# First batch's first MLP: two token pieces of 256 and 320, or two halves of 288 in one tile over two PSUM banks

## The chip, the cores and the metric

The kernel runs on one core of one Trainium2 chip. The metric is device time in microseconds of one execution, the median over several. Five engines work side by side, each in the order of its own queue: TensorE (PE, with its weight loads as PEld), VectorE (DVE), ScalarE (ACT), GpSimd (POOL) and SyncE (SP), which issues most of the DMAs.

## What is computed

Three layers follow each other over 4 batches of 576 tokens, so 2304 tokens in all:

```
k_m, v_m = softmax(phi)^T k, softmax(phi)^T v        per batch and head: 32 memory rows
attn     = softmax(q k_m^T / 8) v_m                  8 heads of 64 -> x of width 512
h        = x @ w_in                                  512 -> 2048
x2       = (h * sigmoid(h)) @ w_out                  2048 -> 512
out      = top-2 of 8 experts over x2, each relu(x2 @ w1[e]) @ w2[e], weighted by the routing
```

The change lies in the second layer, the first MLP, of the first batch only. All values are fp32; a matrix product is made of three products of fp32r parts, high by high, high by low and low by high.

## The kernel before

**Stages.** The first batch's attention comes first. Then the first MLP runs over the batches in steps, and the attention of the next batch, the projection of w_in through v_m, and the routing are hung between the steps as hooks. After the fourth batch the experts run to the end. The weights w_in and w_out arrive as 64-bit values, and during the first batch they are narrowed to fp32 on ACT, DVE and POOL (lines 209 to 232) and split into high and low parts (lines 263, 264, 275, 276). So the first batch's steps carry work on these three engines that later batches don't have.

**A step of the first MLP.** A step s belongs to batch s // 32 and to a block f of 128 rows of the 2048 hidden ones. Each block has two steps, i = 0 with tokens 0 to 255 and i = 1 with tokens 256 to 575. `mlp_h` (line 280) makes 6 matmuls into a PSUM tile `h` of one bank, of which there are two (line 288). Then ACT makes a tanh from PSUM (line 291), DVE multiplies and adds with a second read of PSUM (line 293), which gives twice h * sigmoid(h), ACT copies 256 columns as the high part `gh` (line 297) and DVE or POOL subtracts it for the low part `gl` (line 298). In the first batch POOL has this subtraction in every fourth step, that is for i = 0 of the even blocks. The last 64 tokens of i = 1 go to `gc` the same way (lines 306, 307). When line 293 is done, PE may write that bank again.

**The second product.** `mlp_x` (line 316) runs LAG = 4 steps later and takes block f's `gh` and `gl` as moving data of 512 columns: 6 matmuls a step at line 313, into four PSUM banks that are held for the whole batch. Two more banks, `aux`, serve everything else, so that all 8 are taken.

**Order.** The kernel is written step by step (the loop at the end of `body`: `run_x`, `run_h`, then the hooks), and a scheduler then sets each engine's order from the program, the buffers and its own costs. `issue_after` pins a few places. On the chip each engine runs its list strictly in order.

Of the kernel before, what the change touches and what calls it, by code (L numbers as in the profile page):

```python
# [6 lines left out]
F32 = mybir.dt.float32  # L7
F32R = mybir.dt.float32r
# [3 lines left out]
AF = mybir.ActivationFunctionType  # L12
OP = mybir.AluOpType
AX = mybir.AxisListType

B, H, S, D, M = 4, 8, 576, 64, 32
# [13 lines left out]
MAIN = 512  # L30
NOWHERE = 65536
LAG = 4
# [12 lines left out]
def body(ctx, tc, a):  # L45
    nc = tc.nc
    pe, act, dve, pool, sp = nc.tensor, nc.scalar, nc.vector, nc.gpsimd, nc.sync

    const = ctx.enter_context(tc.tile_pool(name="const", bufs=1))
    ps = ctx.enter_context(tc.tile_pool(name="ps", bufs=2, space=bass.MemoryType.PSUM))  # L50
# [2 lines left out]
    tab_d = tc.dram_tile([E * NS, 2], I32, name="tab_d")  # L53
    xs_d = [tc.dram_tile([CAP, DM], F32, name=f"xs_d{i}") for i in range(2)]

    def psum(tag, bufs):
        return ps.tile([128, 512], F32, name=tag, tag=tag, bufs=bufs)

    ji = const.tile([128, 128], I32, name="ji")
    pool.iota(ji, pattern=[[1, 128]], base=0, channel_multiplier=-1)  # L60
# [15 lines left out]
    m1 = moe1.enter_context(tc.tile_pool(name="m1", bufs=1))  # L76
# [3 lines left out]
    QT, KV, KX, PH, KVT, AH, AU = {}, {}, {}, {}, {}, {}, {}  # L80
# [34 lines left out]
    def phi_max(b, g):  # L115
        r = slice(g * 128, (g + 1) * 128)
        pt = psum("aux", 2)
        pe.transpose(pt[:, :SC], MX.pop((b, g)), ident)
        mt = ap_.tile([128, 1], F32, name="mt")
        dve.tensor_reduce(mt, pt[:, :SC], axis=AX.X, op=OP.max)  # L120
        pb = psum("aux", 2)
        pe.matmul(pb[:SC, :128], mt.to_broadcast([128, SC]), ident, start=True, stop=True)
        for c0, c1 in ((0, 2), (2, NCH)):
            e = PH[b][:, c0:c1, r]
            dve.tensor_sub(e, e, pb[:SC, None, :128].to_broadcast([SC, c1 - c0, 128]))
            last = act.activation(e, e, AF.Exp)
        return last

    def memory(b, g):
        pk = psum("aux", 2)  # L130
        for c in range(NCH):
            for h in range(4):
                j = (4 * g + h) * M

                kv = KV[b, 2 * g + h // 2][:, c, h % 2, :] if c < 4 else KX[b, g][:, h % 2, :]
                pe.matmul(pk[h * M:(h + 1) * M, :130], PH[b][:, c, j:j + M], kv, start=(c == 0), stop=(c == NCH - 1))
        rs = ap_.tile([128, 1], F32, name="rs", bufs=2)
        dve.tensor_scalar(rs, pk[:, 128:129], 1e-9, None, op0=OP.add)
        dve.reciprocal(rs, rs)
        v, w = src[:, :, g, :], pk[:, :128].rearrange("p (t d) -> p t d", t=2)  # L140
        if b == 0:
            act.activation(v, w, AF.Copy, scale=rs)
        else:
            dve.tensor_scalar(v, w, rs, None, op0=OP.mult)
# [90 lines left out]
    WP, WI, ST = {}, {}, {}  # L235
# [42 lines left out]
    G, X2, GC = {}, {}, {}  # L278

    def mlp_h(b, f, i):  # L280
        t0, w = T0[i], TW[i]
        hi, lo = WP[(b * NP + f // 2) // 2]
        c = (f % 4) * 128
        p = psum("h", 2)
        n = 0
        for g in range(2):
            for wt, at in ((hi, 0), (hi, 1), (lo, 0)):
                pe.matmul(p[:, :w], wt[:, g, c:c + 128], AH[b, g][at][:, t0:t0 + w], start=(n == 0), stop=(n == 5))  # L288
                n += 1
        th = m1.tile([128, 320], F32, name="th", bufs=2)  # L290
        act.activation(th[:, :w], p[:, :w], AF.Tanh, scale=0.5)  # L291
        u = th
        dve.scalar_tensor_tensor(u[:, :w], th[:, :w], 1.0, p[:, :w], op0=OP.add, op1=OP.mult)  # L293
        if i == 0:
            G[b, f] = [m1.tile([128, MAIN], F32R, name=f"g{x}", bufs=LAG // 2 + 1) for x in "hl"]
        gh, gl = (x[:, i * 256:(i + 1) * 256] for x in G[b, f])
        act.activation(gh, u[:, :256], AF.Copy)  # L297
        last = (pool if b == 0 and (2 * f + i) % 4 == 0 else dve).tensor_sub(gl, u[:, :256], gh.bitcast(F32))  # L298
        if b:
            LATEST[0] = last  # L300
        if i == 1:
            if (b // 2, f) not in GC:
                GC[b // 2, f] = [m1.tile([128, 128], F32R, name=f"gc{f}_{x}") for x in range(2)]
            ch, cl = GC[b // 2, f]
            r = slice((b % 2) * 64, (b % 2) * 64 + 64)
            act.activation(ch[:, r], u[:, 256:], AF.Copy)
            dve.tensor_sub(cl[:, r], u[:, 256:], ch[:, r].bitcast(F32))

    def accumulate(key, terms, f):
        if f == 0:  # L310
            X2[key] = psum("x2", 4)
        for n, (held, moved) in enumerate(terms):
            pe.matmul(X2[key], held, moved, start=(f == 0 and n == 0), stop=(f == NF - 1 and n == 2))  # L313
# [575 lines left out]
    def at(s, fn, *args):  # L889
        hooks.setdefault(s, []).append((fn, args))  # L890
# [6 lines left out]
    for f in range(1, NF):  # L897
        at(max(0, 2 * f - 5), fetch_wout, f)
        at(2 * f - 1, narrow_wout, f)
    SB = 2 * NF  # L900
    at(8, routing_setup)
    for b in range(1, B):
        s = (b - 1) * SB
        at(s + (1 if b > 1 else 4), load_phi, b)
# [25 lines left out]
        for i in range(0, NP, 2):  # L930
            for x in range(2):
                at(s + SB - 8 + 4 * i, fetch_win, b * NP + i + x)
            at(s + SB - 4 + 4 * i, project, b * NP + i, 2)
    for b in range(B - 1):
        s = (b + 1) * SB + LAG
        for d in range(4):
# [5 lines left out]
        if b == 1:  # L942
# [3 lines left out]
            at(s + 6, tile_d, j)  # L946
    s = 3 * SB
    at(s, open_a)
    at(s - SB + 10, clear)
    for j in range(EARLY):  # L950
# [4 lines left out]
    total = B * SB  # L955
# [1 line left out]
        mlp_x(s // SB, s % SB // 2, s % 2)  # L957

    def run_h(s):
        if s < total:  # L960
            mlp_h(s // SB, s % SB // 2, s % 2)

    def run_hooks(s):
# [16 lines left out]
    s = 0  # L980
    while s < total + LAG + 6:
        if LAG <= s < total + LAG:
            run_x(s - LAG)
        run_h(s)
        run_hooks(s)
        if s in (2 * SB, 4 * SB):
            b = s // SB - 1
            for i in range(1, LAG):
                run_x(s - LAG + i)
                run_hooks(s + i)  # L990
                if s == total and i > 1:
                    main_a(b, 2 * i - 4)
                    main_a(b, 2 * i - 3)
            if s < total:
                cut = (0, 2, 6, 11, NF)
                for i in range(1, LAG + 1):
                    mlp_rest(b, range(cut[i - 1], cut[i]))
                    if i < LAG:
                        run_h(s + i)
                tile_a(TILES.index((b, 4)))  # L1000
                run_hooks(s + LAG)
            else:
                mlp_rest(b, range(0, 2))
                main_c(b)
                mlp_rest(b, range(2, 4))
                main_d(b)
                mlp_rest(b, range(4, 10))
                late = gate(13, 17)()
                late(13, 15)
                for g in range(2):  # L1010
                    main_rows(b, g)
                mlp_rest(b, range(10, NF))
                for fn in (tile_a, tile_b, tile_c, tile_d):
                    fn(17)
            s += LAG - 1
# [55 lines left out]
```

## Time and profile before

| what | us |
|---|---|
| median of 3 runs (845.02 to 845.68) | 845.61 |
| the profiled execution, its own time | 845.91 |
| its span, first to last instruction | 844.1 |
| PE busy in the span | 807.1 (96%) |
| DVE busy | 496.8 (59%) |
| ACT busy | 360.8 (43%) |
| POOL busy | 209.9 (25%) |

A busy share is an average over stages with different limits. PE's matmuls overlap, so that a PE that is busy all the time need not be one at its peak. In the trace a matmul of the change's kind stands at line 288, its tanh at 291, the multiply-add at 293, copy and subtraction at 297 and 298, those of the last 64 tokens at 306 and 307, and the second product at 313.

### The profile page before, as it was taken

The numbers are of one execution on the slowest core, as the hardware profiler recorded it, in microseconds if no ns is written. First come the engines' busy times: TensorE is split into PE (matmuls) and PEld (weight loads), VectorE is DVE, ScalarE is ACT, GpSimd is POOL, SyncE is SP. The second block draws the span as 40 slices with busy tenths as digits, with TensorE's granted clock in tenths as the row PEclk, the third lists the DMA queues.
The fourth block names the chain that finished last, engine by engine and source line by source line (L and its number), as shares of the span: only waits on it lengthen the run. The fifth ranks groups of instructions, "written<-read, shape, count | busy, mean of one in ns | idle before, by whom it ended". The sixth has DMA issues, their size and how long they took to land.

```text
span 844.1 us, 14185 instructions
## 1 busy us (share of the span) xinstructions
PE 807.1 (96%) x5260; PEld 691.4 (82%) x5260; DVE 496.8 (59%) x1178; ACT 360.8 (43%) x856; POOL 209.9 (25%) x237
## 2 busy tenths in 40 slices
PE   4589999999999999999999999999999999999996
PEld 2267678878887888887988989989989899898995
DVE  4898996884268747655724555354553654546521
ACT  3689975444333454553414433324332333233410
POOL 1254530021000400400541504215133142241301
PEclk9599999999999999999999999999999999999999
DMA  9889852543074215232456893765748647586201
GB/s 304 291 295 325 283 217 71 159 131 94 7 229 153 51 51 151 57 82 50 113 138 187 257 257 124 185 237 171 188 169 221 241 139 160 198 220 196 74 4 53
DMA packets 85935, 137.84 MB, mean 163 GB/s; under 512 B 14045, under 2 KB 48349, under 8 KB 85856
## 3 DMA queue, kind: packets, MB, share of 16 engines
q1 hardware_dynamic: 74656, 104.41, 40.9%
q0 software_dynamic: 11200, 32.43, 12.7%
q8 instruction: 43, 0.70, 0.4%
q14 instruction: 36, 0.29, 0.1%
HBM read 106.13 MB, written 31.26 MB: 163 GB/s over the span
## 4 chain that ended last, share of the span: by engine, by line
PE 81%; DVE 9%; ACT 4%; DMA 3%; issue 2%; POOL 1%; SPq 0%; POOLq 0%; ACTq 0%; DVEq 0%
PE x L706 25%; PE x L313 18%; PE x L682 13%; PE h L682 12%; PE h L288 9%; PE aux L157 2%; DMA st<-moe_w_out 1%; DVE th L293 1%; DVE gl L298 1%; DMA kx<-kx 1%; ACT lw L211 1%; POOL wo L232 1%; DMA st<-moe_w_in 1%; DVE mx L113 1%; DVE wo L217 1%
## 5 line engine op out<-in xcount | busy, mean ns | idle before, releaser
L706 PE MATMUL x<-w,gh 128*128 128x512 f32 (+1 forms) x608 | 188.1, 390 | 0.0
L706 PEld LDWEIGHTS x<-w,gh 128*128 128x128 f32 (+1 forms) x608 | 112.4, 186 | 24.3
L682 PE MATMUL h<-xh,w 128*128 128x304 f32 (+4 forms) x512 | 118.7, 304 | 0.0
L706 PE MATMUL x<-w,gl 128*128 128x512 f32 (+1 forms) x304 | 118.5, 390 | 0.0
L682 PE MATMUL x<-xh,w 128*128 128x304 f32 (+4 forms) x512 | 118.1, 302 | 0.0
L288 PE MATMUL h<-ah,wph 128*128 128x320 f32 (+1 forms) x512 | 109.3, 302 | 3.8 <-DVE th L293 1.7
L313 PE MATMUL x<-gh,woh 128*128 128x512 f32 x256 | 105.5, 412 | 0.0
L288 PEld LDWEIGHTS h<-ah,wph 128*128 128x128 f32 x512 | 90.0, 192 | 18.2 <-ACT ah L195 3.6
L721 POOL DMA_INDIRECT out<-y,tab x40 | 41.9, 1049 | 243.1 <-DVE y L716 187.3
L313 PE MATMUL x<-gl,woh 128*128 128x512 f32 x256 | 100.7, 393 | 0.7 <-DVE gl L298 0.7
L313 PE MATMUL x<-gh,wol 128*128 128x512 f32 x256 | 101.2, 395 | 0.0
L293 DVE SCALAR_TENSOR_TENSOR th<-th,h 128x256 f32<-128x256 f32 (+1 forms) x128 | 57.6, 450 | 53.0 <-ACT th L291 52.5
L497 POOL DMA_INDIRECT tab_d<-rows,slot x36 | 40.6, 1128 | 191.3 <-DVE slot L494 177.9
L682 PEld LDWEIGHTS h<-xh,w 128*128 128x128 f32 x512 | 87.3, 188 | 0.6
L682 PEld LDWEIGHTS x<-xh,w 128*128 128x128 f32 x512 | 87.4, 188 | 0.0
L291 ACT ACTIVATE th<-h 128x256 f32<-128x256 f32 (+1 forms) x128 | 52.3, 408 | 73.4 <-PE h L288 71.3
L288 PE MATMUL h<-ah,wpl 128*128 128x256 f32 (+1 forms) x256 | 76.6, 300 | 2.3 <-DVE wpl L264 2.3
L682 PE MATMUL x<-xl,w 128*128 128x304 f32 (+4 forms) x256 | 78.0, 305 | 0.0
L682 PE MATMUL h<-xl,w 128*128 128x304 f32 (+4 forms) x256 | 77.7, 303 | 0.0
L297 ACT ACTIVATE gh<-th 128x256 fp32r<-128x256 f32 x128 | 53.3, 416 | 55.7 <-DVE th L293 55.3
L298 DVE TENSOR_TENSOR gl<-th,gh 128x256 fp32r<-128x256 f32 x120 | 55.1, 459 | 32.0 <-ACT gh L297 28.1
L716 DVE SCALAR_TENSOR_TENSOR y<-x,tab,ex 128x512 f32<-128x512 f32 (+2 forms) x35 | 26.2, 749 | 71.4 <-PE x L706 71.4
(189 smaller groups left out, 1342.0 us busy)
## 6 DMA issues: line engine op xcount, KB each, us to landing
w2s<-moe_w SPq DMA_DIRECT2D x32, 512.0 KB, 8.5
wi<-win_d SPq DMA_DIRECT2D x24, 512.0 KB, 5.1
w1s<-moe_w SPq DMA_DIRECT2D x24, 512.0 KB, 6.2
kv<-kv SPq DMA_DIRECT2D x16, 520.0 KB, 7.3
st<-moe_w_in SPq DMA_DIRECT2D x16, 512.0 KB, 5.2
st<-moe_w_out SPq DMA_DIRECT2D x16, 512.0 KB, 5.9
xs_d<-ex SPq DMA_DIRECT2D x25, 256.0 KB, 3.6
x_d<-xs SPq DMA_DIRECT2D x36, 128.0 KB, 2.4
```

Source lines behind the costliest of these rows:

```text
L157: pe.matmul(p[g][h * M:(h + 1) * M], KVT[b][r, t, h * M:(h + 1) * M], moving(h)[r], start=True, stop=True)
L288: pe.matmul(p[:, :w], wt[:, g, c:c + 128], AH[b, g][at][:, t0:t0 + w], start=(n == 0), stop=(n == 5))
L291: act.activation(th[:, :w], p[:, :w], AF.Tanh, scale=0.5)
L293: dve.scalar_tensor_tensor(u[:, :w], th[:, :w], 1.0, p[:, :w], op0=OP.add, op1=OP.mult)
L297: act.activation(gh, u[:, :256], AF.Copy)
L298: last = (pool if b == 0 and (2 * f + i) % 4 == 0 else dve).tensor_sub(gl, u[:, :256], gh.bitcast(F32))
L313: pe.matmul(X2[key], held, moved, start=(f == 0 and n == 0), stop=(f == NF - 1 and n == 2))
L497: st = pool.indirect_dma_start(out=tab_d, out_offset=bass.IndirectOffsetOnAxis(ap=slot[:, j, k:k + 1], axis=0), in_=rows.bitcast(I32)[:, j ...
L682: pe.matmul(p[:, :w], wt[:, d, c], x[:, d, r], start=(n == 0), stop=(n == 11))
L706: mm = pe.matmul(p, g, w[:, f, :], start=(n == 0), stop=(n == (15 if both else 23)))
L716: done = dve.scalar_tensor_tensor(y, p[:P], w, EX[k, j], op0=OP.mult, op1=OP.add)
L721: st = pool.indirect_dma_start(out=a["out"], out_offset=bass.IndirectOffsetOnAxis(ap=TAB[k][:P, j, 0:1], axis=0), in_=y, in_offset=None, b ...
```

## The change

In the first batch, from step 4 on (block 2 of 16), `mlp_h0` replaces the two calls of `mlp_h` of a block by one at the block's first step. It makes 12 matmuls of 288 columns into one tile `hh` of two banks, six into each, then one tanh over 576 columns, one multiply-add over 576, one copy and one subtraction over 512, and the pair of 64 as before. POOL has the subtraction in every fourth block, 4, 8 and 12. The tile `hh` has one buffer. The two banks change hands by pools that are opened and closed at step 4 and at the end of the batch; blocks 0 and 1 and the other batches are as before.

```diff
--- before.py
+++ after.py
@@ -53,8 +53,20 @@
     tab_d = tc.dram_tile([E * NS, 2], I32, name="tab_d")
     xs_d = [tc.dram_tile([CAP, DM], F32, name=f"xs_d{i}") for i in range(2)]
 
+
+    PH2 = []
+
+    def part(name):
+        if PH2:
+            PH2.pop().close()
+            PH2.pop()
+        pool_of = ExitStack() if name != "ph2" else ctx
+        PH2[:] = [pool_of.enter_context(tc.tile_pool(name=name, bufs=1, space=bass.MemoryType.PSUM)), pool_of]
+
+    part("ph0")
+
     def psum(tag, bufs):
-        return ps.tile([128, 512], F32, name=tag, tag=tag, bufs=bufs)
+        return (PH2[0] if tag == "h" else ps).tile([128, 512], F32, name=tag, tag=tag, bufs=bufs)
 
     ji = const.tile([128, 128], I32, name="ji")
     pool.iota(ji, pattern=[[1, 128]], base=0, channel_multiplier=-1)
@@ -287,7 +299,7 @@
             for wt, at in ((hi, 0), (hi, 1), (lo, 0)):
                 pe.matmul(p[:, :w], wt[:, g, c:c + 128], AH[b, g][at][:, t0:t0 + w], start=(n == 0), stop=(n == 5))
                 n += 1
-        th = m1.tile([128, 320], F32, name="th", bufs=2)
+        th = m1.tile([128, S], F32, name="th", bufs=2)[:, :320]
         act.activation(th[:, :w], p[:, :w], AF.Tanh, scale=0.5)
         u = th
         dve.scalar_tensor_tensor(u[:, :w], th[:, :w], 1.0, p[:, :w], op0=OP.add, op1=OP.mult)
@@ -305,6 +317,29 @@
             r = slice((b % 2) * 64, (b % 2) * 64 + 64)
             act.activation(ch[:, r], u[:, 256:], AF.Copy)
             dve.tensor_sub(cl[:, r], u[:, 256:], ch[:, r].bitcast(F32))
+
+    def mlp_h0(f):
+
+        hi, lo = WP[f // 4]
+        c = (f % 4) * 128
+        p = PH2[0].tile([128, 2, 512], F32, name="hh", bufs=1)
+        for i in range(2):
+            n = 0
+            for g in range(2):
+                for wt, at in ((hi, 0), (hi, 1), (lo, 0)):
+                    pe.matmul(p[:, i, :S // 2], wt[:, g, c:c + 128], AH[0, g][at][:, i * S // 2:(i + 1) * S // 2],
+                              start=(n == 0), stop=(n == 5))
+                    n += 1
+        u = m1.tile([128, S], F32, name="th", bufs=2)
+        v, w = u.rearrange("p (i t) -> p i t", i=2), p[:, :, :S // 2]
+        act.activation(v, w, AF.Tanh, scale=0.5)
+        dve.scalar_tensor_tensor(v, v, 1.0, w, op0=OP.add, op1=OP.mult)
+        gh, gl = G[0, f] = [m1.tile([128, MAIN], F32R, name=f"g{x}", bufs=LAG // 2 + 1) for x in "hl"]
+        act.activation(gh, u[:, :MAIN], AF.Copy)
+        (pool if f % 4 == 0 else dve).tensor_sub(gl, u[:, :MAIN], gh.bitcast(F32))
+        ch, cl = GC[0, f] = [m1.tile([128, 128], F32R, name=f"gc{f}_{x}") for x in range(2)]
+        act.activation(ch[:, :64], u[:, MAIN:], AF.Copy)
+        dve.tensor_sub(cl[:, :64], u[:, MAIN:], ch[:, :64].bitcast(F32))
 
     def accumulate(key, terms, f):
         if f == 0:
@@ -898,6 +933,7 @@
         at(max(0, 2 * f - 5), fetch_wout, f)
         at(2 * f - 1, narrow_wout, f)
     SB = 2 * NF
+    JOIN = 4
     at(8, routing_setup)
     for b in range(1, B):
         s = (b - 1) * SB
@@ -957,7 +993,12 @@
         mlp_x(s // SB, s % SB // 2, s % 2)
 
     def run_h(s):
-        if s < total:
+        if s in (JOIN, SB):
+            part("ph1" if s < SB else "ph2")
+        if JOIN <= s < SB:
+            if s % 2 == 0:
+                mlp_h0(s // 2)
+        elif s < total:
             mlp_h(s // SB, s % SB // 2, s % 2)
 
     def run_hooks(s):
```

What the scheduler makes of it is seen in the order of the instructions.

VectorE's order, block 4 before (the names: `th` is the tanh tile that the multiply-add overwrites, `wo` and `wi` the weights being narrowed, `wol` the low part of w_out, `phi` and `mt` the second batch's attention):

```order
L293 SCALAR_TENSOR_TENSOR th<-th,h 128x256
L120 TENSOR_REDUCE mt<-aux 128x1
L276 TENSOR_TENSOR wol_109<-wo,woh_93 128x512
L125 TENSOR_TENSOR phi<-phi,aux 128x2x128
L217 SCALAR_TENSOR_TENSOR wi<-wi,lw 128x512
L293 SCALAR_TENSOR_TENSOR th<-th,h 128x320
L221 SCALAR_TENSOR_TENSOR wi<-st,wi 128x512
L217 SCALAR_TENSOR_TENSOR wi<-wi,lw 128x512
L298 TENSOR_TENSOR gl<-th,gh 128x256
L221 SCALAR_TENSOR_TENSOR wi<-st,wi 128x512
L307 TENSOR_TENSOR gc_1_716<-th,gc_0_715 128x64
```

The same place on VectorE now, from block 4's multiply-add to block 5's:

```order
L336 SCALAR_TENSOR_TENSOR th<-th,hh 128x576
L233 SCALAR_TENSOR_TENSOR wi<-st,wi 128x512
L229 SCALAR_TENSOR_TENSOR wi<-wi,lw 128x512
L342 TENSOR_TENSOR gc_1_654<-th,gc_0_653 128x64
L233 SCALAR_TENSOR_TENSOR wi<-st,wi 128x512
L137 TENSOR_TENSOR phi<-phi,aux 128x2x128
L229 SCALAR_TENSOR_TENSOR wo<-wo,lw 128x512
L137 TENSOR_TENSOR phi<-phi,aux 128x3x128
L336 SCALAR_TENSOR_TENSOR th<-th,hh 128x576
```

The two multiply-adds have become one, and since POOL has block 4's whole subtraction, no `gl` stands in VectorE's list for it.

TensorE's order before, between two calls of `mlp_h` (`x` are the banks of the second product, `ah` the attention's halves, `wph` and `wpl` the projected weights):

```order
L288 MATMUL h<-ah_299,wpl 128x320
L313 MATMUL x_476<-gh,woh_90 128x512
L313 MATMUL x_476<-gh,wol_106 128x512
L313 MATMUL x_476<-gl,woh_90 128x512
L313 MATMUL x_480<-gh,woh_90 128x512
L313 MATMUL x_480<-gh,wol_106 128x512
L313 MATMUL x_480<-gl,woh_90 128x512
L288 MATMUL h<-ah_295,wph 128x256
```

TensorE's order now, between block 2 and block 3:

```order
L330 MATMUL hh<-ah_302,wpl 128x288
L348 MATMUL x_479<-gh,woh_93 128x512
L348 MATMUL x_479<-gh,wol_109 128x512
L348 MATMUL x_479<-gl,woh_93 128x512
L348 MATMUL x_483<-gh,woh_93 128x512
L348 MATMUL x_483<-gh,wol_109 128x512
L348 MATMUL x_483<-gl,woh_93 128x512
L169 MATMUL aux<-wi,kvt 32x256 x4
L330 MATMUL hh<-ah_298,wph 128x288
```

Before, the second `h` goes to the other bank; now the next `hh` takes the same two banks. Here six matmuls of the second product and four small ones stand between; between most later blocks it is twelve of the second product. From the second batch on the lists of PE, ACT and DVE are the same. On POOL's list seven subtractions of 256 columns have become three of 512. On SP's list the load of the third batch's `phi` now stands ahead of two loads of `wi` that it followed.

## Rows read from the trace of the kernel before

**Rows 1.** Stretches, us: PE, PEld, DVE, ACT, POOL busy (x), PEclk, DMA share, GB/s.

```profile
41.00:129.00 88.00, 81.00 (x602) 61.92 (x603) 81.67 (x156) 75.11 (x177) 40.03 (x36) 1.00 0.80 274
129.00:147.00 18.00, 18.00 (x136) 14.74 (x136) 10.70 (x26) 10.19 (x30) 0.00 (x0) 1.00 0.24 72
```

**Rows 2.** Waits of PE, 41 to 129 us: waited for; us, times, longest.

```profile
PE h L288 <- DVE wpl L264: 2.3, 2, 1.2
PE h L288 <- DVE th L293: 1.7, 3, 0.8
PE h L288 <- DVE ah L196: 0.3, 1, 0.3
```

**Rows 3.** Waits of DVE, 41 to 129 us.

```profile
DVE th L293 <- ACT th L291: 2.0, 3, 1.0
```

**Rows 4.** Chain that ended last, 129 to 139 us: start, us, what.

```profile
129.26 1.39 PE x L313 x6
130.65 0.87 PE h L288 x6
...
132.91 0.71 PE h L288 x6
...
137.98 1.02 PE aux L157 x32
```

**Rows 5.** Timeline of DVE and POOL: start us, us, engine, line, operation.

```profile
45.31 0.41 DVE L298 TENSOR_TENSOR gl<-th,gh 128x256 fp32r<-128x256 f32 x1
45.64 0.47 DVE L293 SCALAR_TENSOR_TENSOR th<-th,h 128x320 f32<-128x320 f32 x1
...
45.83 1.31 POOL L276 TENSOR_TENSOR wol<-wo,woh 128x512 fp32r<-128x512 f32 x1 [1.51 <-ACT woh L275]
...
46.04 1.64 DVE L217 SCALAR_TENSOR_TENSOR wo<-wo,lw 128x512 int32<-128x512 int32 x1
...
55.30 0.21 DVE L307 TENSOR_TENSOR gc<-th,gc 128x64 fp32r<-128x64 f32 x1
...
55.43 0.40 DVE L293 SCALAR_TENSOR_TENSOR th<-th,h 128x256 f32<-128x256 f32 x1
...
55.76 0.41 DVE L264 TENSOR_TENSOR wpl<-aux,wph 128x256 fp32r<-128x256 f32 x1
...
73.64 0.69 DVE L276 TENSOR_TENSOR wol<-wo,woh 128x512 fp32r<-128x512 f32 x1
...
74.25 0.69 DVE L221 SCALAR_TENSOR_TENSOR wi<-st,wi 128x512 int32<-128x512 int32 x1
```

**Rows 6.** Groups by line, 41 to 129 us: busy us, mean ns, idle before.

```profile
L298 DVE TENSOR_TENSOR gl<-th,gh 128x256 fp32r<-128x256 f32 x23 | 14.3, 623 | 1.1 <-ACT gh L297 0.8
...
L307 DVE TENSOR_TENSOR gc<-th,gc 128x64 fp32r<-128x64 f32 x15 | 8.1, 539 | 0.0
```

**Rows 7.** Groups by line of POOL, 41 to 129 us.

```profile
L232 POOL TENSOR_TENSOR wo<-wo,cg 128x512 f32<-128x512 f32 x15 | 18.4, 1226 | 8.0 <-DVE wo L217 4.2 <-ACT th L291 1.5 <-ACT cg L227 1.3
L276 POOL TENSOR_TENSOR wol<-wo,woh 128x512 fp32r<-128x512 f32 x8 | 10.9, 1358 | 7.8 <-ACT woh L275 7.1 <-DVE wo L217 0.7
L298 POOL TENSOR_TENSOR gl<-th,gh 128x256 fp32r<-128x256 f32 x7 | 7.3, 1045 | 19.0 <-ACT gh L297 19.0
```

**Rows 8.** Timeline of ACT at 45 us.

```profile
44.82 0.41 ACT L297 ACTIVATE gh<-th 128x256 fp32r<-128x256 f32 x1
45.13 0.62 ACT L275 ACTIVATE woh<-wo 128x512 fp32r<-128x512 f32 x1
...
45.65 0.67 ACT L227 ACTIVATE cg<-st 128x512 bf16<-128x512 f32 x1
```

**Rows 9.** Groups by line of ACT, 41 to 129 us.

```profile
L291 ACT ACTIVATE th<-h 128x320 f32<-128x320 f32 x16 | 6.9, 432 | 1.8 <-PE h L288 1.4 <-DVE gc L307 0.4
```

**Rows 10.** Timeline of SP's queue about 120 us.

```profile
112.81 7.42 SPq L244 DMA_DIRECT2D wi<-win_d  x3
122.21 0.33 SPq L87 DMA_DIRECT2D phi<-phi  x1
```

## The prediction

> **What bounds the kernel now.** The page comes first: PE is busy for 96% of the span, so only a stretch in which PE waits can give anything back. The view by stretches finds it. From 41 to 129 us, where the first batch's blocks run, DVE is busy for 81.67 of 88.00 us, PE for 81.00, ACT for 75.11 and POOL for 40.03; from 129 to 147 us PE has all 18.00 us and DVE 10.70 [rows 1]. The reader is to see two engines close to full in the first stretch, and one in the second. The waits say which leads: PE waits for DVE, 2.3 us for `wpl`, 1.7 us for the multiply-add, 0.3 us for `ah` at the very end [rows 2]. DVE itself is idle for 88.00 - 81.67 = 6.33 us, the largest part of it, 2.0 us, for ACT's tanh [rows 3]. So DVE sets the pace up to about 129 us with PE close behind; after that the chain is PE alone [rows 4]. A microsecond taken from DVE before 129 us is a microsecond of the kernel, as long as PE still has waits to give up, and PE has 88.00 - 81.00 = 7.00 us of them.
>
> **The change part by part.** It touches 14 blocks, 2 to 15.
>
> *PE.* Six matmuls of 256 columns take 0.71 us and six of 320 take 0.87 [rows 4]; 12 of 288 columns are as many columns, so 0.71 + 0.87 = 1.58 us before and after. Nothing.
>
> *DVE, multiply-add.* What counts is from start to start, because neighbours overlap. The one of 256 columns starts at 55.43 and its neighbour at 55.76: 0.33 us. The one of 320 starts at 45.64 and its neighbour at 46.04: 0.40 us [rows 5]. Before, a block pays 0.73. The 64 columns between them cost 0.07, so 576 columns cost about 0.40 + 256 * 0.07 / 64 = 0.68 us (an estimate from these two). Saved: 0.05 a block, 14 * 0.05 = 0.70 us.
>
> *DVE, subtraction.* 256 columns go from 45.31 to 45.64, 0.33 us; the row with 512 columns and the same kinds of operands goes from 73.64 to 74.25, 0.61 us [rows 5]. Before, POOL had 7 of these 28 halves and DVE 21: 21 * 0.33 = 6.93 us. Now POOL has 3 blocks and DVE 11: 11 * 0.61 = 6.71. Saved: 0.22 us. Copy and subtraction of the last 64 tokens stay. DVE together: 0.92 us.
>
> The rows give 0.05 us for an instruction less. [...] The start times show that neighbours overlap by about 0.08 us, so I keep 0.92.
>
> *POOL against DVE.* When POOL runs an operation of two inputs from SBUF, such an operation of DVE is held until POOL is done: `wo` at 46.04 takes 1.64 us while POOL works from 45.83 for 1.31 us, and other rows of 512 columns take 0.69 [rows 5]. So `gl` has a mean of 623 ns where a free one has 410, and `gc` 539 where a free one has 210 [rows 5, 6]: 23 * 0.213 + 15 * 0.329 = 9.8 us lost on these two lines. POOL's operations of this kind take 18.4 + 10.9 + 7.3 = 36.6 us [rows 7]. Seven of 1.045 become three of about 1.36 (the 512 columns of line 276): 7.3 - 4.1 = 3.2 us less, 9% of the 36.6. I take 9% of the 9.8, 0.9 us. Bounds: 0, if DVE never meets just these, and 3.2, if it meets them always.
>
> *ACT.* The copies of 256 columns start 0.31 us before their neighbour (44.82 to 45.13), the one of 512 takes 0.52 (45.13 to 45.65) [rows 8]: 0.10 a block, 1.4 us over 14. The tanh I leave at no saving. ACT is not the pace, but it ends DVE's idle time [rows 3]; I count 0.3 of the 1.4, between 0 and 1.4.
>
> *Queues.* POOL's list gets shorter; its own idle before these rows is 19.0 us [rows 7], so nothing comes of that. On SP two loads of `wi` now stand behind `phi`, which went out at 122.21, instead of among those from 112.81 on [rows 10]. The projection that reads them is at 137.98 [rows 4], over 15 us later, and hides it; without that cover each would cost PE its wait.
>
> *The single tile.* Before, the next `h` went to the other bank; now PE may not begin a block until the multiply-add over all 576 columns is done. That wait is new and has no row. Beneath it lie twelve matmuls of the second product, 2 * 1.39 = 2.78 us [rows 4]. The tanh is about 0.432 + 0.21 = 0.64 us (256 more columns, by 0.62 - 0.41 of the copies [rows 8, 9]) and the multiply-add 0.68: 1.32 us. So 1.46 us of queueing on ACT and DVE together is covered. One ACT copy ahead (0.52) and one DVE subtraction ahead (0.61) are 1.13 and fit. I take 0; the bounds are 0 and the second rival's price. No gain can come of it, since it only adds a wait.
>
> Sum: 0.92 + 0.9 + 0.3 = 2.1 us. The profiled execution took 845.91 us, of which its span is 844.1, so it would take 843.8. It stands 0.3 above the median of 845.61; against the median I predict **843.5 us**. What is late next is `ah`, already the last wait of PE in the stretch [rows 2], and then PE itself.
>
> **The rivals.**
>
> *The saving turns into DVE's idle time (no change).* A wide tanh ends 0.64 - 0.43 = 0.21 us later than the one of 320, and DVE cannot begin before. DVE waited for a tanh only 3 times [rows 3]; if it now waits in every block, that is 14 * 0.21 = 2.9 us, more than the saving; in half the blocks 1.5 us, and the time is 843.5 + 1.5 = 845.0. For: ACT is busy for 85% [rows 1] and often late. Against: DVE has other work in its list between two multiply-adds, seven operations between blocks 4 and 5.
>
> *PE waits for its one tile (slower).* Decided where tanh and multiply-add stand behind more than 1.46 us of other work. A DVE operation that POOL holds is enough together with one ACT copy: 1.64 + 0.52 = 2.16 us [rows 5, 8], 0.7 too much. Between blocks 2 and 3 the new order leaves only six matmuls of the second product, 1.39 us, and four small ones, so there PE must wait. Nothing absorbs it, because PE is 92% busy: in half the blocks 7 * 0.7 = 4.9 us, and with the saving 843.5 + 4.9 = 848.4. For: PE already waited 3 times for a multiply-add with two banks [rows 2]. Against: those were 1.7 us in 88. [...]
>
> *More than forecast (faster).* If POOL's shorter time is met always (3.2 instead of 0.9) and ACT's 1.4 us count whole, the saving is 0.92 + 3.2 + 1.4 = 5.5 us and the time 840.1. For: the losses to POOL are the largest waste in the stretch. Against: PE has only 7.00 us to give, and waits for several things.
>
> That the change doesn't do what it says is excluded: the order shows one multiply-add and one subtraction a block.
>
> **How the numbers follow.** A measurement of this kernel can tell about 0.2%, 1.7 us, from no change: faster is below 843.9, slower above 847.3. The forecast has 0.35, the larger saving 0.10, no change 0.30, the single tile 0.25. So faster 0.45, same 0.30, slower 0.25. The likeliest case alone ranges from 842.0 to 843.9. Eight times in ten the time should lie between **841.0** (short of the larger saving's end) and **848.5** (about the price of the single tile; the worse half of that rival is left out).
>
> **What would show it.** Right: line 336 at about 0.75 us of duration in 14 instructions, line 339 at about 0.69 where POOL is idle, DVE's idle time over the same blocks still near 6 us, and the run of PE that now stands at 129.26 [rows 4] about 2 us earlier. PE's waits for the multiply-add would stay below 3 us. Wrong: PE waiting more than 5 us in all for line 336, or ACT waiting for `hh`, means the single tile; DVE idle by 2 us more behind the tanh of line 335 means the first rival; a mean of `gl` and `gc` near the free ones means the larger saving. A change after 147 us would be none of this.

## The result and the profile after

The changed kernel takes **850.5 us** (median of 5 runs, 850.33 to 851.88), beside 845.61 for the kernel before in the same job: ratio 1.0065, 95% interval 1.0053 to 1.0077. It is slower by 0.65%, more than the 0.2% that can be told apart. The forecast was 843.5, its range ended at 848.5, and the sign is wrong. The profiled execution took 850.33 us, its span is 848.5.

Where the time went shows when the same work is looked up in both traces. The table gives the start of the n-th matmul of the second product (line 313 before, 348 after); it is made from the PE timelines.

| n | 49 | 73 | 109 | 151 | 163 | 175 | 199 |
|---|---|---|---|---|---|---|---|
| before, us | 65.89 | 81.07 | 97.65 | 119.69 | 124.17 | 129.10 | 138.94 |
| after, us | 66.14 | 82.65 | 100.93 | 122.94 | 130.56 | 134.02 | 143.85 |
| later by | 0.25 | 1.58 | 3.28 | 3.25 | 6.39 | 4.92 | 4.91 |

The loss builds up from about 70 us on and is complete at 134 us; from there on the distance is constant. So the changed blocks lose it, and nothing behind them. The stretches of the changed kernel that answer to [rows 1], with the same columns:

```profile
41.00:134.00 93.00, 83.03 (x602) 61.59 (x603) 83.21 (x134) 74.38 (x150) 35.88 (x32) 1.00 0.77 259
134.00:147.00 13.00, 13.00 (x106) 10.58 (x108) 5.99 (x16) 7.89 (x23) 0.00 (x0) 1.00 0.18 55
```

The stretch lasts 5 us longer, and no engine's busy time grew by as much. DVE has 22 instructions fewer (156 to 134), yet it is busy for 83.21 us instead of 81.67, and idle for 93.00 - 83.21 = 9.79 instead of 6.33. Both are the wrong way round. The granted clock of TensorE is 1.00 in both kernels, so it has no part in this trace. DVE's groups by line over the same stretch show where its busy time is (busy us, mean ns, idle before and what ended most of it):

```profile
L229 DVE SCALAR_TENSOR_TENSOR wo<-wo,lw 128x512 int32<-128x512 int32 x15 | 14.7, 983 | 2.0 <-ACT wo L224 1.1 <-ACT lw L223 0.8
L336 DVE SCALAR_TENSOR_TENSOR th<-th,hh 128x576 f32<-128x576 f32 x14 | 10.4, 744 | 0.0
L339 DVE TENSOR_TENSOR gl<-th,gh 128x512 fp32r<-128x512 f32 x11 | 10.3, 935 | 2.0 <-ACT gh L338 1.8
L229 DVE SCALAR_TENSOR_TENSOR wi<-wi,lw 128x512 int32<-128x512 int32 x10 | 8.0, 805 | 1.9 <-ACT wi L224 1.0 <-ACT lw L223 0.8
...
L342 DVE TENSOR_TENSOR gc<-th,gc 128x64 fp32r<-128x64 f32 x14 | 6.7, 476 | 0.3 <-ACT gc L341 0.3
...
L319 DVE TENSOR_TENSOR gc<-th,gc 128x64 fp32r<-128x64 f32 x2 | 1.4, 704 | 0.0
```

The multiply-add costs what was forecast (744 ns) and has no idle time before it. The joining of the weights' low and high parts, `wo`, has a mean of 983 ns where a free one takes 0.69 us (its median is 693 ns). In the kernel before the same line, over 41 to 129 us, stood so:

```profile
L217 DVE SCALAR_TENSOR_TENSOR wo<-wo,lw 128x512 int32<-128x512 int32 x15 | 11.4, 757 | 1.1 <-ACT wo L212 0.9
```

The longest DVE instruction of the stretch is one that should be short. Timeline of the changed kernel, DVE and POOL at 90 us, and ACT behind them:

```profile
90.25 2.78 DVE L342 TENSOR_TENSOR gc<-th,gc 128x64 fp32r<-128x64 f32 x1
...
90.52 1.30 POOL L339 TENSOR_TENSOR gl<-th,gh 128x512 fp32r<-128x512 f32 x1
...
91.77 1.17 POOL L244 TENSOR_TENSOR wo<-wo,cg 128x512 f32<-128x512 f32 x1
...
92.95 0.68 DVE L229 SCALAR_TENSOR_TENSOR wo<-wo,lw 128x512 int32<-128x512 int32 x1
...
93.67 0.68 ACT L223 ACTIVATE lw<-st 128x512 int32<-128x512 uint32 x1 [1.22 <-DVE wo L229]
```

`gc` needs 0.21 us where POOL is silent (at 49.20 in the kernel before, with POOL idle from 49.00 to 50.61). Here it takes 2.78, while POOL's new wide subtraction and `wo` run back to back. ACT is idle for 1.22 us behind it, since `lw` has one buffer, and two PE waits of 1.4 and 0.9 us follow at 94 us. The waits of PE, DVE and ACT over 41 to 134 us (waited for; us, times, longest) answer to [rows 2, 3]:

```profile
PE hh L330 <- DVE th L336: 2.8, 4, 1.0
PE hh L330 <- DVE wpl L276: 1.9, 3, 0.9
PE hh L330 <- ACT wph L275: 1.4, 1, 1.4
PE aux L169 <- DVE phi L137: 1.2, 1, 1.2
PE hh L330 <- DVE ssm L194: 0.9, 1, 0.9
PE h L300 <- DVE th L305: 0.8, 1, 0.8
```

```profile
DVE ah L208 <- ACT ah L207: 1.9, 1, 1.9
DVE gl L339 <- ACT gh L338: 1.8, 2, 1.1
...
DVE wi L229 <- ACT lw L223: 0.8, 2, 0.5
DVE wo L229 <- ACT lw L223: 0.8, 1, 0.8
```

```profile
ACT woh L287 <- POOL wo L244: 4.7, 10, 0.7
ACT lw L223 <- DVE wo L229: 4.4, 6, 1.2
ACT ah L207 <- PE hh L330: 1.9, 1, 1.9
```

PE's waits for the multiply-add grew from 1.7 us to 4.5: 2.8 at the new tile, 0.9 that is put down to `ssm`, which runs right behind a multiply-add, and 0.8 in the first two blocks, a wait that the 1.7 us of before hold too. All of PE's waits over 0.15 us together grew from 6.8 us to 10.5. ACT waits 4.4 us for DVE's join of the weights, where the kernel before had 0.7. The copy of `ah` waits 1.9 us for PE: its tile has three buffers, and the one it wants is free only when the last block's 12 matmuls are done. That wait is late in the stretch. PE's own last wait ends at 124.46 us, and from there on PE is never idle (columns as in [rows 1]):

```profile
124.50:134.00 9.50, 9.50 (x63) 7.84 (x64) 6.80 (x12) 4.66 (x9) 0.00 (x0) 1.00 0.53 181
```

So DVE's 2.7 us of idle time in these 9.5 us, 1.9 for `ah` and 0.7 for a `gh`, cost the kernel nothing: PE sets the pace there.

**A budget.** To compare kernels I take DVE from ACT's second copy `woh` (about 45 us) to the 175th matmul of the second product, and split the time in three. *Held* is what DVE instructions take above the median of their line and tile, over the whole execution, while a two-input operation of POOL runs (counted from 0.15 us on). *Idle* is idle. *Work* is the rest.

| us | stretch | work | held | idle |
|---|---|---|---|---|
| before | 83.97 | 67.44 | 10.37 | 6.16 |
| after | 89.29 | 67.03 | 12.50 | 9.76 |
| difference | +5.3 | -0.4 | +2.1 | +3.6 |

The joined instructions do save DVE work, but 0.4 us of it, and held and idle time grow by 5.7. How the 5.7 is split depends on where the stretch ends, since DVE does not set the pace in its last part. Up to PE's last wait after the change (124.46 us), and up to the place of the kernel before from which PE has as much work left (119.2 us), held time goes from 8.5 to 12.5 us and idle time from 5.6 to 7.1, at 60 us of work in both.

### The profile page after: what moved, and what is told of

Its sections match the earlier page's. It is cut to its first block, busy times and chain, and to the rows that moved or that the text cites. A ratio compares the mean times of both kernels' runs of the same rounds, so it can differ in the third digit from the quotient of the medians.

```text
span 848.5 us, 14114 instructions
## 1 busy us (share of the span) xinstructions
PE 808.2 (95%) x5260; PEld 690.2 (81%) x5260; DVE 498.4 (59%) x1154; ACT 359.6 (42%) x828; POOL 204.5 (24%) x233
## 3 DMA queue, kind: packets, MB, share of 16 engines
q0 software_dynamic: 11200, 32.43, 12.7%
## 5 line engine op out<-in xcount | busy, mean ns | idle before, releaser
L300 PE MATMUL h<-ah,wph 128*128 128x256 f32 (+1 forms) x400 | 85.3, 302 | 2.4 <-ACT ah L207 1.6
L300 PEld LDWEIGHTS h<-ah,wph 128*128 128x128 f32 x400 | 70.8, 193 | 13.0 <-ACT ah L207 3.6
L305 DVE SCALAR_TENSOR_TENSOR th<-th,h 128x256 f32<-128x256 f32 x100 | 45.2, 452 | 52.8 <-ACT th L303 52.3
L303 ACT ACTIVATE th<-h 128x256 f32<-128x256 f32 x100 | 41.0, 410 | 73.2 <-PE h L300 71.1
L741 PEld LDWEIGHTS x<-w,gl 128*128 128x128 f32 (+1 forms) x304 | 56.4, 186 | 12.7
L309 ACT ACTIVATE gh<-th 128x256 fp32r<-128x256 f32 x100 | 41.7, 417 | 53.1 <-DVE th L305 52.6
L348 PEld LDWEIGHTS x<-gh,woh 128*128 128x128 f32 x256 | 48.2, 188 | 18.2 <-issue 9.9
```

The source lines that it names most:

```text
L741: mm = pe.matmul(p, g, w[:, f, :], start=(n == 0), stop=(n == (15 if both else 23)))
```

## The experiments

Two readings stand against each other. By the first, the change costs its 5 us itself: one tile for PE, wide operations, POOL's wide subtraction, the `lw` buffer. By the second, what the change does itself is small, and the kernel before has an order of its lists that is better than most: any edit that makes the engines' lists come out differently loses some tenths of a per cent. Where an expectation gives a theory a letter or a name, it says what that is. Ratios are to the kernel before in the same job.

### First: the change taken apart

The kernel before, with only copy and subtraction joined to 512 columns (both halves keep their own tile and step):

```diff
+        v = TH[f][:, t0:t0 + w]
+        act.activation(v, p[:, :w], AF.Tanh, scale=0.5)
+        dve.scalar_tensor_tensor(v, v, 1.0, p[:, :w], op0=OP.add, op1=OP.mult)
+        if i:
...
+            act.activation(gh, u[:, :MAIN], AF.Copy)
+            (pool if f % 4 == 0 else dve).tensor_sub(gl, u[:, :MAIN], gh.bitcast(F32))
```

> Kernel before, with only copy and subtraction of a block joined to 512 columns (POOL takes blocks 4, 8, 12); the two pieces of 256 and 320 keep a bank each, their own steps, and their own tanh and multiply-add. One tile theory (the loss is PE waiting for its one tile): no loss, 844.5 to 846. Wide operations theory (a joined operation comes too late or holds DVE too long): most of the 4.9 us remains, over 848. POOL theory (the 512-column subtraction on POOL holds DVE): 847 to 848.

Measured 1.0033 (1.0020 to 1.0045). The expectations of these first four runs are in us for a kernel before of 845.6; on the chip where they ran it took 850.4, so they are to be read as ratios to it. 1.0033 would be 848.4: not "no loss", and just above the limit of the wide operations.

The kernel before, with both halves issued in the block's first step and nothing joined:

```diff
+        if 4 <= s < SB:
+            if s % 2 == 0:
+                mlp_h(0, s // 2, 0)
+                mlp_h(0, s // 2, 1)
```

> Kernel before, with both pieces of a block written at its first step, into their two banks; nothing joined. Order theory (twelve matmuls in one go and the second piece a step early upset the three engines' lists): 849 to 851. One tile theory: each bank still comes free by its own multiply-add, 844.5 to 847.

Measured 1.0022 (1.0009 to 1.0036), or 847.5, between the two forecasts: a small loss with nothing joined.

The changed kernel's tile and matmuls, with all four operations by halves:

```diff
+        for i in range(2):
+            act.activation(v[:, i], w[:, i], AF.Tanh, scale=0.5)
+            dve.scalar_tensor_tensor(v[:, i], v[:, i], 1.0, w[:, i], op0=OP.add, op1=OP.mult)
...
+            act.activation(gh[:, r], u[:, r], AF.Copy)
+            (pool if (2 * f + i) % 4 == 0 else dve).tensor_sub(gl[:, r], u[:, r], gh[:, r].bitcast(F32))
```

> The changed kernel's one tile over two banks and its twelve matmuls in one go, but tanh, multiply-add, copy and subtraction by halves, as many instructions as before. One tile theory: the loss stays and the saved fixed costs come back, 850.5 to 852. Wide operations theory: back to 845 to 847.

Measured 1.0087 (1.0070 to 1.0104), more than either theory had. PE waits 2.7 us for the multiply-add here, and 0.3 us in the run before this one; but most of the growth is DVE's held time, 16.7 us, beside an idle time of 6.6.

The changed kernel with all subtractions on DVE:

```diff
-        (pool if f % 4 == 0 else dve).tensor_sub(gl, u[:, :MAIN], gh.bitcast(F32))
+        dve.tensor_sub(gl, u[:, :MAIN], gh.bitcast(F32))
```

> The changed kernel with the three subtractions of POOL given to DVE. POOL theory: at least 2 us faster than the changed kernel, below 848.5. One tile theory: DVE has 3 * 0.61 = 1.8 us more and loses less to POOL, 850 to 852.

Measured 1.0065 (1.0046 to 1.0085), as the changed kernel and as the one tile theory had it. Held time fell by 5.1 us, to 7.4, and idle time rose by 5.4, to 15.2. But 5.8 us of that idle time lies behind PE's last wait, which ends at 123.67 us, and there TensorE's granted clock had fallen to half while PE worked without a gap (columns as in [rows 1]):

```profile
124.10:130.90 6.80, 6.80 (x31) 4.47 (x30) 4.22 (x8) 2.60 (x5) 0.00 (x0) 0.50 0.69 227
```

With a granted clock of 0.50 a matmul of 256 columns took 0.23 us in the kernel before (three from 38.67 to 39.36 us), with 1.00 it took 0.12 (six in 0.71 us [rows 4]). So at the full clock PE would need about half of these 6.8 us, and up to 3.4 us of this execution may be the clock's (an estimate from these two). This run does not settle what POOL's wide subtraction costs.

Next, both kernels unchanged on another chip, the changed kernel with a tile for each half, and the changed kernel joined in blocks 2 to 8 alone:

```diff
-        p = PH2[0].tile([128, 2, 512], F32, name="hh", bufs=1)
+        p = [psum("h", 2) for i in range(2)]
```

```diff
-    JOIN = 4
+    JOIN, APART = 4, 18
```

> The kernel before, unchanged, for a profile beside the others of this call. Every theory: within 0.2% of the runs of the kernel before, and a granted clock that falls in the same places as in the other profiles of this chip, if it falls at all.

> The changed kernel, unchanged, beside the others. Every theory: a ratio of 1.0065 to the kernel before.

> The changed kernel, both halves of 288 at the block's first step, but a tile of one bank for each half with its own tanh and multiply-add; copy and subtraction joined. One tile theory: the two runs that differ in the tile alone (e2, e3) put it at 5 us, so this is at least 2 us faster than the changed kernel, ratio 1.002 to 1.005. If what e2 lost (0.22%) and e1 lost (0.33%) add up: 1.0055. Order theory alone: 1.0065 again.

> The changed kernel's blocks 2 to 8 only; blocks 9 to 15 as before. If each block costs the same: half the loss, 1.003. If the loss arises where the second batch's softmax loads DVE (blocks 10 to 15): 1.000 to 1.001. If it arises where the weights are narrowed: 1.005 to 1.0065.

The kernel before gave 848.97 us and the same budget as in its first trace (held 10.3, idle 6.2): the stretch repeats from chip to chip. The changed kernel gave 1.0080 (1.0061 to 1.0099), with two tiles 1.0062 (1.0045 to 1.0079), and joined in seven blocks 1.0063 (1.0043 to 1.0083). So blocks 2 to 8 alone lose most of it or all, within the 1.005 to 1.0065 that was expected if the loss arises where the weights are narrowed. The medians of one tile and two lie 0.2% apart and the intervals overlap: two tiles do not bring the loss back, and what they are worth is not settled (the traces also differ by a fall of TensorE's granted clock to half, 3.4 us with one tile and 6.8 with two). With narrow operations the two runs that differ in the tile (and in halves of 288 for 256 and 320) lay further apart, 1.0087 against 1.0022. With two tiles PE waits less for the multiply-add in these blocks (1.1 and 0.2 us) and more for the projection's low part `wpl` (3.4 us, where the changed kernel on this chip waited 1.9):

```profile
PE aux L169 <- DVE wpl L276: 2.2, 2, 1.9
PE h L330 <- DVE wpl L276: 1.2, 2, 0.8
PE h L300 <- DVE th L337: 1.1, 1, 1.1
...
PE h L330 <- DVE th L337: 0.2, 1, 0.2
```

### Second: the suspected waits one by one, and a rearrangement that joins nothing

Wide tanh and multiply-add with narrow copies; then ACT's low part written back into the staged words, so that the buffer `lw` is gone, in both kernels; then the kernel before with POOL's subtractions moved by a block:

```diff
-        low = ap_.tile([128, 512], I32, name="lw", bufs=1)
+        low = t[:, :, 0]
```

```diff
-        last = (pool if b == 0 and (2 * f + i) % 4 == 0 else dve).tensor_sub(gl, u[:, :256], gh.bitcast(F32))
+        last = (pool if b == 0 and (2 * f + i) % 4 == 2 else dve).tensor_sub(gl, u[:, :256], gh.bitcast(F32))
```

> The changed kernel with copies and subtractions of gh and gl by halves of 256 as before, POOL with 7 of them; the single tile, the wide tanh and the wide multiply-add stay. Theory A (what is joined is cheap, the single tile costs): as the changed kernel, ratio 1.006 to 1.008. Theory B (the lists of ACT and DVE lose their fit where wide operations come, a wide copy above all; the copies joined alone gave 1.003): 1.003 to 1.005. Theory C (the spread of POOL's small operations holds DVE): as the narrow one-tile kernel, 1.009, with over 15 us of DVE held between 45 us and the 174th matmul of the second product, against 10.4 in the kernel before and 12.5 in the changed one.

> The changed kernel, but ACT writes the low part of a weight back into the staged words, so the one buffer lw is gone and ACT need not wait for DVE's join of the piece before (4.4 us of ACT's waits in the changed kernel's stretch, 0.7 in the kernel before). Theory B (the loop between ACT and DVE over that buffer makes the idle time): DVE idle from 9.8 to 7 or less, ratio 1.002 to 1.004. Theory A (the single tile): nothing changes, 1.006 to 1.008. Both would have it 0.3 % worse if an operand with a stride of 8 bytes makes DVE's join slower.

> The kernel before with the same step: no buffer lw. In the kernel before ACT waited for that buffer 0.7 us only, so both theories expect 0.999 to 1.001 from the wait. If DVE's join gets slower by the stride, or if any change of the lists costs something in this stretch, 1.002 to 1.004.

> The kernel before with POOL's subtractions of the first batch's blocks moved by one block: condition 2 instead of 0, 8 of 32 as before. Nothing is joined, no tile is shared. Theory A and the sum of the prediction: 0.999 to 1.001, since no engine's work changes. Theory D (the order of the kernel before is a favourable one of many, and every rearrangement of its lists falls back by some tenths of a per cent through held and idle DVE time): 1.002 to 1.005.

Wide tanh with narrow copies: 1.0068 (1.0054 to 1.0082), as the changed kernel and as theory A had it: with the single tile and the wide tanh the loss is there without the joined copies. Without `lw`: 1.0116 (1.0100 to 1.0131) for the changed kernel and 1.0061 (1.0047 to 1.0075) for the one before. Both miss every theory's range. The wait for `lw` is gone, the join is as fast as ever (median 682 ns against 693), and others stand in its place. ACT's waits in the changed kernel without `lw`, 41 to 138 us:

```profile
ACT woh L287 <- POOL wo L244: 4.7, 6, 1.1
ACT st L223 <- DMA st<-moe_w_in: 3.8, 3, 3.0
ACT ah L207 <- DVE att L200: 3.2, 1, 3.2
ACT th L335 <- PE hh L330: 2.9, 2, 2.0
ACT st L223 <- DMA st<-moe_w_out: 2.8, 3, 2.0
```

The staged words are now in use until the join has read them, so the next loads start later: 3.8 + 2.8 us of waiting for loads, where the changed kernel had 0.5. The buffer was no useless one. In the kernel before without `lw` all of the loss comes behind the 145th matmul of the second product, which starts at 113.98 us, a microsecond earlier than before (114.99). The granted clock was at half from 120.3 to 127.1 us, and PE was busy for 6.60 of these 6.80 us. So an unknown part of this loss, up to 3.4 us by the same estimate, is the clock's.

The fourth run is the control. It joins nothing, shares no tile and gives POOL the same 8 halves, only one block on, and it takes 1.0051 (1.0038 to 1.0065). Its stretch, with the columns of [rows 1], and its longest wait of DVE over 41 to 131 us:

```profile
41.00:131.00 90.00, 83.34 (x598) 63.55 (x592) 77.04 (x153) 74.05 (x174) 39.52 (x37) 0.98 0.78 267
```

```profile
DVE wol L276 <- ACT woh L275: 5.5, 5, 1.6
```

POOL holds DVE for 2.3 us less than in the kernel before (8.1), but the subtraction of the weights now waits 5.5 us for ACT's copy, where it waited 1.6 before, and DVE is idle for 12.2.

### Third: both kernels rearranged

One such run could be bad luck. So the kernel before was rearranged in two more ways (POOL takes the second half of the even blocks; the narrowing of w_out's rows comes a step later), and the changed one in two as well (POOL in blocks 5, 9, 13; the narrowing a step later):

```diff
-        last = (pool if b == 0 and (2 * f + i) % 4 == 0 else dve).tensor_sub(gl, u[:, :256], gh.bitcast(F32))
+        last = (pool if b == 0 and (2 * f + i) % 4 == 1 else dve).tensor_sub(gl, u[:, :256], gh.bitcast(F32))
```

```diff
-        at(2 * f - 1, narrow_wout, f)
+        at(2 * f, narrow_wout, f)
```

```diff
-        (pool if f % 4 == 0 else dve).tensor_sub(gl, u[:, :MAIN], gh.bitcast(F32))
+        (pool if f % 4 == 1 else dve).tensor_sub(gl, u[:, :MAIN], gh.bitcast(F32))
```

> The kernel before with POOL subtracting the second 256 columns of every other block instead of the first: 8 halves of 32 as before, nothing joined. Theory D (every rearrangement of the lists of the kernel before falls back): 1.002 to 1.006, as the other one (1.0051), with DVE's held and idle time between 45 us and the 174th matmul of the second product together 2 to 5 us above its 16.5. Theory A (the loss is the change's own, the one rearrangement so far was an unlucky one): 0.998 to 1.002.

> The kernel before with the narrowing of each row of the second weight one step later (behind the first half of its block instead of ahead of it). The same work in another order. Theory D: 1.002 to 1.006. Theory A: 0.998 to 1.002, or worse only if the second product waits for woh and wol, which would be seen as waits of PE at line 313.

> The changed kernel with POOL's 3 wide subtractions in blocks 5, 9, 13 instead of 4, 8, 12. Theory D (a new order draws anew from the same spread; what the change does itself is small): any value from 1.000 to 1.008, as likely below 1.0065 as above. Theory A (the single tile and the wide operations cost their 5 us in any order): 1.006 to 1.008, with DVE's held and idle time about 22 us again.

> The changed kernel with the narrowing of each row of the second weight behind its block instead of ahead of it. Theory D: any value from 1.000 to 1.008, and within 0.003 of the kernel before with the same step. Theory A: the kernel before with the same step plus 0.0065.

The two rearrangements of the kernel before take 1.0067 (1.0050 to 1.0084) and 1.0123 (1.0106 to 1.0140), those of the changed one 1.0034 (1.0020 to 1.0048) and 1.0136 (1.0120 to 1.0153). So moving POOL's three subtractions gives back half of the loss, and with the narrowing a step later both kernels lose the same within 0.0013, less than either interval is wide. That loss is also larger than anything the change does, and above the range that either theory gave for the kernel before; of the wait at line 313 that theory A had named for more, PE has 0.6 us. The last two runs looked for a better order of the changed kernel: POOL in blocks 3, 7, 11 and 15 (`f % 4 == 3`), and POOL in blocks 5, 9 and 13 with the blocks up to 4 left in halves:

```diff
-        (pool if f % 4 == 0 else dve).tensor_sub(gl, u[:, :MAIN], gh.bitcast(F32))
+        (pool if f % 4 == 1 else dve).tensor_sub(gl, u[:, :MAIN], gh.bitcast(F32))
...
-    JOIN = 4
+    JOIN = 10
```

> The changed kernel with POOL's wide subtractions in blocks 3, 7, 11 and 15 (4 instead of 3). Theory D (the order decides): anything from 1.000 to 1.008; the best phase so far, blocks 5, 9 and 13, gave 1.0034. Theory A (the change costs its 5 us in any order; 1.0034 was luck): 1.006 to 1.008.

> The changed kernel joined from the sixth row block on only, the blocks up to 4 in halves as before, with POOL's wide subtractions in blocks 5, 9 and 13. Up to the 60th matmul or so of the second product it has the order of the kernel before; behind it the better one of the two phases. Theory D: 1.000 to 1.004, and 0.998 if the joined work is worth its 0.4 us and no new wait comes. Theory A: the share of its 11 of 14 blocks, 1.005.

Measured 1.0058 (1.0042 to 1.0075) and 1.0020 (1.0008 to 1.0031). The second is the best order of joined work that was found; it is still slower than the kernel before. No run beats the kernel before.

All orders side by side; held, idle and their sum are DVE's, from the budget, in us:

| kernel | ratio | held | idle | sum |
|---|---|---|---|---|
| before | 1 | 10.4 | 6.2 | 16.5 |
| before, POOL a block on | 1.0051 | 8.1 | 12.2 | 20.3 |
| before, POOL on second halves | 1.0067 | 12.4 | 8.9 | 21.3 |
| before, without `lw` | 1.0061 | 11.8 | 9.6 | 21.3 |
| before, narrowing later | 1.0123 | 13.0 | 12.8 | 25.7 |
| before, both halves early | 1.0022 | 11.6 | 7.4 | 19.0 |
| before, copies joined | 1.0033 | 9.9 | 10.5 | 20.4 |
| after | 1.0065 | 12.5 | 9.8 | 22.3 |
| after, joined from block 5, POOL 5, 9, 13 | 1.0020 | 10.9 | 8.3 | 19.2 |
| after, POOL 5, 9, 13 | 1.0034 | 11.2 | 8.4 | 19.6 |
| after, POOL 3, 7, 11, 15 | 1.0058 | 10.4 | 11.3 | 21.8 |
| after, all on DVE | 1.0065 | 7.4 | 15.2 | 22.6 |
| after, without `lw` | 1.0116 | 9.7 | 17.4 | 27.1 |
| after, narrowing later | 1.0136 | 12.4 | 15.6 | 28.0 |
| after, second chip | 1.0080 | 12.7 | 10.1 | 22.8 |
| after, two tiles | 1.0062 | 10.5 | 10.7 | 21.2 |
| after, blocks 2 to 8 alone | 1.0063 | 11.4 | 8.5 | 19.8 |
| after, narrow copies | 1.0068 | 12.1 | 9.4 | 21.4 |
| after, all narrow | 1.0087 | 16.7 | 6.6 | 23.3 |

The time goes with the sum to within about 2 us, and not with either column alone. In part this is arithmetic, since held, idle and work make up the stretch and work stays between 65 and 69 us. The lowest sum of all is that of the kernel before.

## Why the prediction was wrong, by its own steps

*The bound.* DVE up to 129 us and PE behind it: right, and the loss arose there alone; in the changed kernel DVE sets the pace up to 124.5 us, PE's last wait. But "a microsecond taken from DVE before 129 us is a microsecond of the kernel" failed. DVE has 16.5 us of held and idle time in this stretch, which a new order redistributes, and the order moved more than the work did.

*PE's matmuls, zero.* Right: the last block's twelve start at 128.98 and the second product follows at 130.56, 1.58 us.

*DVE's fewer instructions, -0.92.* The sign is right: the budget has -0.4, and the multiply-add is 744 ns as said. Held time is taken out by a threshold of 0.15 us, so the half microsecond between the two is at the edge of what this can show.

*POOL against DVE, -0.9.* **This is the first step that failed**; the budget has +2.1, and +4.0 up to PE's last wait. The price was made from two lines, and on these it was even too small. `gl` was held for 11 * (0.935 - 0.69) = 2.7 us and `gc` for 14 * (0.476 - 0.21) + 2 * (0.704 - 0.21) = 4.7, together 7.4 instead of 9.8. But POOL's other operations now met other lines: `wo` pays 15 * (0.983 - 0.757) = 3.4 us more than before, `wi` 0.4, and one subtraction of the softmax 1.94 instead of 1.35 us. A share of POOL's busy time says nothing about which DVE instruction stands beside it. The trace of the kernel before had the loss in a pattern: of its 10.4 us held, 3.9 were four short `gc` beside POOL's `wo`, and 4.2 were five `gl` whose holding began beside its `wol`. After the change `wo` of DVE pays 4.5 us, where it had paid 1.0.

*ACT, -0.3.* **The second step that failed**: DVE's idle time was to fall and rose by 3.6 us. The largest waits in it, 1.9 us for `ah` and 0.7 of the 1.8 for `gh`, come behind PE's last wait and cost nothing; up to there idle time rose by 1.5 us. Of the waits that counted, 1.6 us is `lw` (0.2 before). The loop behind `lw` is the one that I had not looked for: ACT's list stands still for DVE's join, and DVE's next join for ACT.

*The single tile, 0.* Too low: a term put at nothing that the trace shows, though not the whole cause that its rival made of it. PE's waits behind the multiply-add rose by 2.8 us (1.7 to 4.5), the largest part of the 3.7 by which all its waits rose; one of them, 0.86 us from 50.7 us on, stands just where the rival had put it, between blocks 2 and 3. The rival's 848.4 is the nearest of the forecast's times, yet with a tile for each half PE waits for other things and the kernel is still at 1.0062. What the second tile is worth here, 1.0080 with one tile against 1.0062 with two, lies within the intervals.

*The other rivals.* Idle time behind a wider tanh did not come: line 336 has no idle time before it. The larger saving did not come either.

*Queues, 0.* Right: PE never waits for `wi`.

What is shown: the work did not grow, and the loss stands in held and idle time of DVE and in PE's waits for it. Taking away the single tile, the joined copies, POOL's wide subtraction or `lw` one at a time does not bring it back. Edits of the kernel before that join nothing lose 0.2 to 1.2%; the two that only move POOL's subtractions lose 0.51 and 0.67%, as much as the change, with no fall of the clock in their traces from 47 us to the end of the stretch. In two pairings of like edits the changed kernel lies 0.17% below the kernel before (POOL a block on) and 0.13% above it (narrowing later); without `lw` it is 0.55% above, unedited 0.65%. So the order of the lists is enough for such a loss; that it is the cause of this one, and the change's own cost nothing, is argued. The single tile can have a share that no run here separates: 0.2% by the medians in the changed kernel, 0.65% between the two narrow runs, which differ in the halves too. Argued only is also that the kernel before stands out because its lists were fitted to just these durations, and why its order is the better one stays open.

## What to carry to other kernels

Where three in-order engines share a stretch and each is 80 to 93% busy, an edit that reorders their lists can move the time by more than the instructions that it saves (here by 0.2 to 1.2%, with no work saved); before crediting a saving there, rearrange the kernel without the saving once and see how far that alone moves it. Price contention between POOL and DVE by pairs that stand beside each other in the order, on all of DVE's lines, not by busy shares. Before calling idle time of an engine a loss, see whether the engine that sets the end still waits for it there. After an edit that saves work in such a stretch, fit the placement anew: here moving three subtractions to other blocks gave back half of the loss.

## What the runs showed of the hardware

*A short DVE operation held over two of POOL's.* The `gc` of 64 columns that started at 90.25 was held through POOL's two operations from 90.52 to 92.94, although its recorded start is ahead of the first one's (recorded spans of POOL are rough). It lost 2.57 us, for an instruction of 0.21. The same `gc` takes 2.86 us on the second chip and 2.88 with seven blocks joined, and one in the kernel before with POOL on second halves takes 2.23 us at 54.00, each over two operations of POOL back to back. Beside one operation of POOL a `gc` took 1.19 us (at 43.20 in the kernel before, with POOL's `wo` from 43.12 to 44.31); in these four DVE was passed over by POOL's next operation too.

*The clock fell behind a wait of PE on one chip, and not on the other.* The changed kernel on its second chip waited at the same place, and for as long, as on the first (1.4 us for `wph`, 0.9 for `wpl`, behind 94 us). On the second chip PE's granted clock then fell to half for 3.4 us. Columns as in [rows 1], the second chip:

```profile
93.50:96.90 3.40, 1.04 (x6) 0.39 (x4) 2.26 (x5) 3.40 (x9) 1.91 (x2) 1.00 1.02 396
97.00:100.30 3.30, 3.30 (x26) 2.42 (x26) 2.96 (x6) 2.26 (x5) 0.48 (x1) 0.50 0.90 240
```

The first chip in the same stretches:

```profile
93.50:96.90 3.40, 1.46 (x7) 0.73 (x5) 2.29 (x5) 3.23 (x8) 1.49 (x2) 1.00 1.01 396
97.00:100.30 3.30, 3.00 (x30) 2.28 (x31) 3.27 (x6) 3.08 (x7) 0.93 (x1) 1.00 0.82 256
```

The stretch of the budget was 89.8 us with the fall and 89.3 without, so it cost little here, where PE waits for DVE again behind it. Where PE no longer waits, as from 124.1 us in the run with all subtractions on DVE, it may have cost up to 3.4 us (the estimate made there). Most of the other variants had such falls of 3.4 or 6.8 us in the stretch of the budget; the changed kernel's first trace, the one with all operations narrow, and the kernel before with POOL's work a block on or on second halves had none from 47 us to its end, and lost 0.5 to 0.9%. So the loss does not need the clock, but the ratios of runs with falls can hold a share of it.
